# A fused attention and MLP block on one core: the start's loads in another order, the keys' weights in two transposed halves, and a new written-out order

## The chip, the cores and the metric

One core of a Trainium2 chip. The time is device microseconds of one execution; the kernel before takes 173.94 us (median of 3 runs, 173.92 to 173.96).

## The reference, cut to what matters

```python
def _A_ref(x, wqkv, w_phi, wo):            # S=2048, D=512, H=32 heads of 16
    qkv = (x @ wqkv).reshape(B, S, 3, H, Dh).transpose(2, 0, 3, 1, 4)
    q, k, v = qkv[0], qkv[1], qkv[2]
    pq = einsum("bhsd,hdf->bhsf", q, w_phi);  pk = einsum("bhsd,hdf->bhsf", k, w_phi)
    phi_q = concatenate([softmax(pq), softmax(-pq)]);  phi_k = the same of pk
    kv  = einsum("bhsf,bhsd->bhfd", phi_k, v);         z = sum of phi_k over s
    num = einsum("bhqf,bhfd->bhqd", phi_q, kv);        den = phi_q . z + 1e-6
    return (num / den) @ wo
def _B_ref(x, w1, b1, w2):                 # F=1792
    h = x @ w1 + b1
    return (h * tanh(softplus(h))) @ w2    # mish
xn = layernorm(x)
return x + _A_ref(xn, ...) + _B_ref(xn, ...)
```

## The kernel before, in words

The 2048 tokens are 16 tiles of 128, in 4 groups of 4. All data is bf16, sums are fp32. Each head's 16x16 feature map is folded into the projection: `fold` (L156) multiplies the transposed columns of `wqkv` (tile `wT`, loaded by a transposing DMA in `load_turned`, L143) with a block-diagonal `Wbd`, so that logits come straight from the normalised tokens. The keys' folded weights are `wkp`, the queries' `wqp`. `wT[:, j, kt*128:...]` is read by fold number `kt`, four matmuls each; folds 0 and 1 read its columns 0 to 255, folds 2 and 3 the others, and these columns are rows of `wqkv`.

Group 0 of the tokens is normalised tile by tile and turned by TensorE (`first_turn`, L560); the later groups are turned by DMA (`ln_turn_dma`, L186). Twelve matmuls on constants (`warm`, L513) stand ahead of everything on TensorE.

The whole order is written out by hand in the string `STEPS`; the schedule is manual, each engine runs its part of the steps in this order, and only semaphores for data and buffers hold it back. A number behind `@` is the PSUM bank (six, numbered 0 to 5; one double bank more is used in turn by wide logits, the accumulation and the attends). The steps:

- `LS i`, `RS i`, `AZ i`, `TP i`, `TC i`: statistics (DVE), reciprocal root (POOL), centring (DVE), turn (TensorE) and copy of tile i of group 0. `LN g`, `AP g k`: the same for group g, the turn by DMA from SP.
- `WB`: `Wbd`. `PB`, `CB`: the bias turned by TensorE (L533) and copied. `KM`: a mask.
- `F0 kt`, `FD kt`: fold of the keys' weights and its copy; `F`, `FC` for the queries. `WT` loads the queries' weights.
- `LP`: first logits, tiles 0 and 1 interleaved (L209). `L s i`, `LC s i`: logits of stage s (0 to 3 keys, 4 to 7 queries), tile i, and their copy. `WL`: two more of them in the double bank. `V t`, `VC t`: values.
- `H u`, `M u`: hidden units, 128 of 1792 for one group, u from 0 to 55, and mish on ScalarE.
- `E s l` extremes for the softmaxes (DVE, l = 0, 1 for the two signs), `X s k` exponential (ScalarE), `S s k` row sums (DVE, L305). Keys: `R` inverse of the sums (`v` on DVE, `a` through logarithm and exponential on ScalarE), `N` normalises, `A g k` accumulates kv. `KV` masks it. Queries: `W` weighs one softmax against the other (they share a denominator) and turns the features by DMA (`turn`, L295, tiles `qT`).
- `Q h i`, `G h i`, `C h`: attend (TensorE), gather to SBUF (ScalarE), division by the denominator (DVE) and a turn by DMA (L458). `O t`: second layer of the MLP, 14 matmuls; `P t`: output projection into the same bank; `Y t`: residual (DVE, L477) and store. `OH`, `PH`, `YH`: the last tile in two parts.
- `DX g`, `DW i`: loads of tokens, of `wo` (3) and `w2` (2).

ScalarE holds one table at a time, that of mish or that of exponential and logarithm; a change loads the other (`table`, L138).

The loads at the start stand ahead of the steps (L483 to L493), most on SP's queue, three on ACT's: `wsrc`, tile 1 of the tokens and the bias.

Of the kernel before, what the change touches and what calls it, by code (L numbers as in the profile page):

```python
# [23 lines left out]
STEPS = """
LS 0; RS 0; DX 2; LS 1; WB; RS 1; AZ 0; TP 0 @0; F0 0 @1; F0 1 @2; AZ 1; FD 0 v; TP 1 @3; TC 1 v; LS
2; PB @4; RS 2; TC 0 a; LS 3; RS 3; FD 1 a; AZ 2; F0 2 @5; F0 3 @0; FD 2 a; FD 3 a; LP i @1,2; KM;
DX 3; AZ 3; V 0 @3; LC 0 0 a; TP 2 @5; V 1 @0; TC 2 a; TP 3 @1; VC 0 a; LC 0 1 v; TC 3 v; CB; L 0 2
@5; L 0 3 @2; LC 0 3 a; LN 1; H 0 @3; H 1 @1; H 2 @4; M 0; LC 0 2 a; H 3 @2; M 1; M 2; M 3; VC 1 a;
E 0 0; H 4 @3; H 5 @5; AP 1 0; H 6 @1; H 7 @4; M 4; H 8 @2; M 5; H 9 @0; M 6; M 7; H 10 @3; M 8; M
9; M 10; AP 1 1; H 11 @5; E 0 1; V 4 @1; X 0 1; WL 1; LN 2; V 6 @4; VC 4 a; X 0 0; L 1 0 @2; L 1 3  # L30
@0; LC 1 0 a; V 5 @3; LN 3; VC 5 a; H 12 @1; WL 2; H 13 @2; VC 6 a; S 0 0; LC 1 3 a; M 11; V 3 @3; M
12; M 13; H 14 @4; H 15 @0; H 16 @5; H 17 @1; VC 3 a; M 14; H 18 @2; M 15; M 16; M 17; LC 1 2 a; H
19 @3; AP 2 0; AP 2 1; AP 3 0; L 2 0 @4; LC 2 0 a; L 2 1 @0; LC 2 1 a; V 2 @5; S 0 1; L 2 2 @1; M
18; LC 1 1 a; M 19; H 20 @4; LC 2 2 a; AP 3 1; H 21 @0; WT; H 22 @2; M 20; VC 2 a; R 0 1 v; L 2 3
@3; H 23 @1; R 0 0 v; N 0 1; M 21; N 0 0; H 24 @4; M 22; LC 2 3 a; F 0 @5; F 1 @0; E 1 0; E 1 1; M
23; M 24; F 2 @2; E 2 0; E 2 1; FC 0 a; H 25 @3; H 26 @1; FC 1 a; H 27 @4; M 25; M 26; L 3 2 @5; FC
2 a; M 27; V 7 @0; L 3 3 @3; V 11 @1; F 3 @2; L 3 0 @4; LC 3 0 v; LC 3 2 a; L 3 1 @5; A 0 0; X 1 0;
X 1 1; A 0 1; LC 3 3 a; FC 3 v; S 1 0; V 8 @4; LC 3 1 a; VC 7 a; L 4 0 @2; E 3 0; VC 8 a; LC 4 0 a;
L 4 1 @3; LC 4 1 a; L 4 3 @5; VC 11 a; L 4 2 @0; X 2 0; V 9 @4; L 5 0 @2; H 28 @3; H 29 @1; VC 9 a;
LC 4 2 v; M 28; M 29; H 30 @0; H 31 @4; H 32 @3; M 30; H 33 @1; H 34 @0; M 31; M 32; M 33; M 34; H  # L40
35 @4; M 35; H 36 @3; M 36; S 1 1; LC 4 3 a; R 1 0 v; E 3 1; LC 5 0 a; N 1 0; R 1 1 v; H 37 @1; H 38
@0; H 39 @4; H 40 @3; H 41 @5; H 42 @2; S 2 0; A 1 0; M 37; N 1 1; M 38; M 39; M 40; A 1 1; M 41; M
42; X 3 0; L 6 3 @1; L 5 2 @0; V 10 @4; VC 10 a; L 5 1 @3; LC 5 2 a; L 6 0 @5; E 4 0; E 4 1; X 2 1;
S 3 0; V 15 @2; VC 15 a; V 13 @4; VC 13 a; LC 6 0 a; R 2 0 a; S 2 1; DW 3; R 3 0 a; X 3 1; L 6 1 @0;
LC 5 1 a; DW 2; N 3 0; N 2 0; L 5 3 @2; O 0 @4; S 3 1; V 12 @5; V 14 @3; LC 6 1 a; LC 5 3 a; O 1 @0;
L 6 2 @2; R 2 1 a; N 2 1; VC 14 a; LC 6 3 a; VC 12 v; R 3 1 a; N 3 1; X 4 0; A 2 0; S 4 0; LC 6 2 a;
A 2 1; A 3 0; W 4 0 v; X 4 1; H 43 @3; M 43; A 3 1; H 44 @1; H 45 @5; M 44; H 46 @2; M 45; H 47 @3;
M 46; M 47; H 48 @1; KV; H 49 @5; H 50 @2; Q 0 0; M 48; M 49; G 0 0; M 50; H 51 @3; H 52 @1; H 53
@5; S 4 1; W 4 1 v; M 51; M 52; H 54 @2; H 55 @3; Q 0 1; M 53; E 5 0; E 5 1; M 54; E 6 0; L 7 0 @1;
M 55; G 0 1; C 0 a; X 5 0; LC 7 0 a; L 7 1 @5; X 5 1; O 2 @2; O 3 @3; LC 7 1 a; L 7 2 @1; LC 7 2 a;  # L50
S 5 0; Q 1 0; L 7 3 @5; G 1 0; E 6 1; W 5 0 a; P 0; P 1; Y 0; Q 1 1; O 4 @1; G 1 1; LC 7 3 a; O 5
@4; S 5 1; Q 2 0; O 6 @5; C 1 a; P 2; G 2 0; W 5 1 v; Y 1; Q 2 1; P 3; O 7 @0; E 7 0; X 6 0; S 6 0;
G 2 1; Q 3 0; C 2 a; G 3 0; Y 2; Y 3; X 6 1; O 8 @2; Q 3 1; W 6 0 v; E 7 1; S 6 1; P 4; P 5; G 3 1;
C 3 a; Q 4 0; X 7 0; Y 4; W 6 1 v; X 7 1; S 7 0; O 9 @3; O 10 @1; G 4 0; Q 4 1; P 6; P 7; G 4 1; Y
5; Y 6; C 4 a; Q 5 0; W 7 0 a; G 5 0; O 11 @4; Q 5 1; Y 7; O 12 @5; S 7 1; G 5 1; C 5 a; Q 6 0; G 6
0; O 13 @0; Q 6 1; G 6 1; W 7 1 v; P 8; P 9; Q 7 0; C 6 a; G 7 0; P 10; P 11; Y 8; Q 7 1; G 7 1; O
14 @2; Y 9; Y 10; C 7 a; P 12; P 13; OH 0 @3; PH 0; Y 11; P 14; OH 1 @1; PH 1; Y 12; Y 13; YH 0; Y
14; YH 1
"""


# [1 line left out]
def kernel(  # L63
# [19 lines left out]
    FT = F // P  # L83
# [53 lines left out]
            tables[0] = name  # L137
            nc.scalar.preload_act_table_set(name)  # L138

    def load_turned(base_col):  # L140
# [2 lines left out]
        nc.sync.dma_start_transpose(out=wT[:], in_=A_wqkv[:, base_col : base_col + D])  # L143
# [345 lines left out]
    nc.sync.dma_start(x_sb[:, 2:4, :], x_v[:, 2:4, :])
    nc.sync.dma_start(wv[:], wqkv_v[:, :, 2 * D : 3 * D])  # L490
# [165 lines left out]
```

## Time and profile before

| | |
|---|---|
| median of 3 runs | 173.94 us (173.92 to 173.96) |
| the profiled execution | 174.0 us |
| its span, first to last instruction | 172.3 us |
| granted TensorE clock | 1.000 |
| TensorE busy | 168.7 us, 1039 matmuls |
| VectorE, ScalarE busy | 143.2 us, 119.5 us |
| moved by DMA | 18.02 MB |

The span is what the profile's views cover; 1.7 us of the execution lie around it. Busy time counts overlapping instructions of one engine once. A matmul's end is modelled and lies some 0.16 us after the start of the next one in a row of back-to-back matmuls. "SPq" and "ACTq" are the DMA issues of these engines; "to landing" is the time from the start of the issue until the data is there.

### The profile page before, as it was taken

Reading aid. Unit: us, or ns where it says so; the run is one execution under the profiler, and the core shown is the slowest. Engines: PE = TensorE matmul, PEld = TensorE weight load, DVE = VectorE, ACT = ScalarE, POOL = GpSimd, SP = SyncE. Lnnn points to the kernel's source line nnn. Section 1 sums busy time; section 2 is a strip of 40 time slices with the busy share of each in tenths; the row PEclk is TensorE's granted clock in tenths of the full one; section 3 lists DMA queues with packets and bytes.
Section 4 is the critical chain, followed back from the end, with each engine's and each line's share of the span. In section 5 each row is a group of like instructions: output and inputs, shape, how many; then the busy total and the mean of one; then the engine's idle time right before and its main releaser. Section 6 shows DMA issues by size and latency. Waiting matters only on the chain.

```text
span 172.3 us, 2713 instructions
## 1 busy us (share of the span) xinstructions
PE 168.7 (98%) x1039; PEld 82.4 (48%) x1039; DVE 143.2 (83%) x221; ACT 119.5 (69%) x192; POOL 9.4 (5%) x26
## 2 busy tenths in 40 slices
PE   8999999999999999999999999999999999999993
PEld 2554444444545444454446544444444545445452
DVE  2878998999997999979999999799988996844433
ACT  2446889979899998989999988974063883414200
POOL 4332205000000000000000000000000000000000
PEclk9999999999999999999999999999999999999999
DMA  5999350199930000000000363023974749885641
GB/s 98 269 377 365 82 98 0 37 189 207 366 120 0 0 4 0 0 0 0 4 0 0 64 118 66 12 51 67 150 152 93 150 95 144 172 168 100 173 134 61
DMA packets 44953, 18.02 MB, mean 105 GB/s; under 512 B 37004, under 2 KB 44940, under 8 KB 44940
## 3 DMA queue, kind: packets, MB, share of 16 engines
q1 hardware_dynamic: 44096, 17.60, 44.5%
q10 hardware_dynamic: 844, 0.25, 0.6%
q8 instruction: 8, 0.13, 0.3%
q14 instruction: 5, 0.04, 0.1%
HBM read 6.84 MB, written 2.10 MB: 52 GB/s over the span
## 4 chain that ended last, share of the span: by engine, by line
PE 95%; DMA 3%; SPq 0%; DVE 0%; issue 0%
PE po L463 28%; PE ph L228 28%; PE pl L194 14%; PE po L470 8%; PE pv L194 8%; DMA wT<-in_A_wqkv_dram 3%; PE pnd L418 2%; PE pkv L387 2%; PE pfold L156 1%; PE pwide L194 1%; PE pl L209 1%; PE ptr L560 0%; SPq L483 0%; DVE x_sb L477 0%; PE pb L533 0%
## 5 line engine op out<-in xcount | busy, mean ns | idle before, releaser
L463 PE MATMUL po<-w_sb,acts 128*128 128x512 bf16 (+2 forms) x238 | 50.7, 366 | 0.0
L228 PE MATMUL ph<-xnT,w_sb 128*128 128x512 bf16 x224 | 50.1, 379 | 0.0
L239 ACT ACTIVATE acts<-ph,b1f 128x512 bf16<-128x512 f32 x56 | 37.2, 694 | 4.6 <-PE ph L228 4.4
L305 DVE TENSOR_REDUCE s<-e 128x128 f32<-128x2048 bf16 x16 | 36.4, 2279 | 2.5 <-ACT e L288 2.5
L228 PEld LDWEIGHTS <-w_sb 128*128 128x128 bf16 x224 | 21.7, 98 | 25.5
L463 PEld LDWEIGHTS <-acts 128*128 128x128 bf16 x238 | 22.3, 98 | 24.1
L288 ACT ACTIVATE e<-e 128x2048 bf16<-128x2048 bf16 x16 | 30.3, 1908 | 0.0
L194 PEld LDWEIGHTS <-xnT 128*128 128x128 bf16 x184 | 17.6, 98 | 20.1 <-DMA wv<-in_A_wqkv_dram 0.2
L252 ACT CAST p_sb<-pl 128x512 bf16<-128x512 f32 x27 | 15.4, 587 | 5.5 <-PE pl L194 4.7
L433 ACT COPY ds<-pnd 128x32 f32<-128x32 f32 x16 | 2.9, 183 | 23.5 <-PE pnd L418 23.5
L194 PE MATMUL pv<-wv,xnT 128*128 128x512 bf16 x64 | 16.1, 379 | 0.0
L477 DVE TENSOR_TENSOR x_sb<-po,x_sb 128x512 bf16<-128x512 f32 (+2 forms) x17 | 10.9, 654 | 5.7 <-PE po L470 5.7
L470 PE MATMUL po<-wqk,xnT 128*128 128x512 bf16 (+2 forms) x68 | 15.5, 366 | 0.0
L194 PE MATMUL pl<-wqk,xnT 128*128 128x512 bf16 x64 | 15.3, 379 | 0.0
L170 DVE BATCH_NORM_STATS2 stats<-x_sb 128x6 f32<-128x512 bf16 x16 | 10.1, 679 | 4.3 <-DMA x_sb<-in_A_x_dram 4.3
L263 DVE TENSOR_TENSOR m<-m 128x512 bf16<-128x512 bf16 (+1 forms) x32 | 11.5, 358 | 1.1
L194 PE MATMUL pl<-wkp,xnT 128*128 128x512 bf16 x48 | 11.7, 379 | 0.0
L263 DVE TENSOR_TENSOR m<-p_sb 128x1024 bf16<-128x1024 bf16 x16 | 10.9, 682 | 0.2 <-ACT p_sb L252 0.2
L272 DVE TENSOR_TENSOR e<-p_sb,m 128x2048 bf16<-128x2048 bf16 x8 | 9.8, 1226 | 1.4 <-PE pkv L387 1.1
L272 DVE TENSOR_TENSOR e<-m,p_sb 128x2048 bf16<-128x2048 bf16 x8 | 9.8, 1225 | 0.3
L340 DVE TENSOR_TENSOR e<-e,r 128x2048 bf16<-128x2048 bf16 x8 | 9.6, 1215 | 0.0
L138 ACT ACT_TABLE_LOAD x7 | 9.0, 1283 | 0.1
(62 smaller groups left out, 131.4 us busy)
## 6 DMA issues: line engine op xcount, KB each, us to landing
out_dram<-x_sb SPq DMA_DIRECT2D x15, 128.0 KB, 2.0
w_sb<-in_B_w_dram SPq DMA_DIRECT2D x2, 896.0 KB, 7.8
x_sb<-in_A_x_dram SPq DMA_DIRECT2D x3, 512.0 KB, 10.0
w_sb<-in_B_w_dram SPq DMA_DIRECT2D x2, 640.0 KB, 8.8
wv<-in_A_wqkv_dram SPq DMA_DIRECT2D x1, 512.0 KB, 4.5
wqk<-in_A_wo_dram SPq DMA_DIRECT2D x1, 512.0 KB, 4.6
w_sb<-in_B_w_dram SPq DMA_DIRECT2D x1, 512.0 KB, 9.6
x_sb<-in_A_x_dram SPq DMA_DIRECT2D x1, 256.0 KB, 3.2
```

Of the source, the lines that this page charges most:

```text
L170: nc.vector.bn_stats(stats[:, i, :], xs[:, i, :])
L194: nc.tensor.matmul(pp, lhsT=xnT[:, t, kt, :], rhs=w[:, kt, :], start=(kt == 0), stop=(kt == KT - 1),)
L228: nc.tensor.matmul(ph_of[u][:], lhsT=w1_sb[:, kt, f * P : (f + 1) * P], rhs=xnT[:, g * TPG : (g + 1) * TPG, kt, :], start=(kt == 0), stop= ...
L239: nc.scalar.activation(acts[:, f, g * 512 : (g + 1) * 512], ph_of.pop(u)[:], ACT.Mish, bias=b1f[:, f : f + 1])
L252: copy(p_of[s][:, i, :], pl_of.pop((s, i)))
L263: nc.vector.tensor_tensor(out=m[:], in0=src[:, :, 0:half], in1=src[:, :, half : 2 * half], op=op)
L272: nc.vector.tensor_tensor(out=e_of[s][:].rearrange("p t j l c -> p (t j) l c")[:, :, pl, :].rearrange("p t (c e o) -> p t c e o", e=8, o=2 ...
L288: nc.scalar.activation(v, v, ACT.Exp)
L305: nc.vector.reduce_sum(t[:], pair(s, k).rearrange("p t j l (c e) -> p (t j l c) e", e=16), axis=AX.X)
L463: nc.tensor.matmul(po_of[t, c.stop][:, c], lhsT=acts[:, f, t * P : (t + 1) * P], rhs=w2_sb[:, f, c], start=(f == 0), stop=False,)
L470: nc.tensor.matmul(po_of[t, c.stop][:, c], lhsT=oT_of[t // 2][:, t % 2 * 4 + j, :], rhs=wo_sb[:, j, c], start=False, stop=(j == 3),)
L477: nc.vector.tensor_tensor(out=y, in0=po_of.pop((t, c.stop))[:, c], in1=y, op=ALU.add)
```

## The change

Three things at the start. SP loads the first four tiles of tokens (0, 1, then 2 and 3 together) ahead of the keys' weights; tile 1 leaves ACT's queue. The keys' weights come in two transpositions of 256 rows of `wqkv`, so that folds 0 and 1 wait for the first alone. And the bias is turned first on TensorE, ahead of tile 0.

```diff
-    def load_turned(base_col):
+    def load_turned(base_col, *rows):
         wT = lnp.tile([P, 4, 512], BF16, name="wT", tag="xn")
-        nc.sync.dma_start_transpose(out=wT[:], in_=A_wqkv[:, base_col : base_col + D])
+        for r in rows:
+            nc.sync.dma_start_transpose(out=wT[:, :, r], in_=A_wqkv[r, base_col : base_col + D])
         return wT
...
-    nc.sync.dma_start(x_sb[:, 0, :], x_v[:, 0, :])
-    wT_of = {0: load_turned(D)}
+    for t in (slice(0, 1), slice(1, 2), slice(2, 4)):
+        nc.sync.dma_start(x_sb[:, t, :], x_v[:, t, :])
+    wT_of = {0: load_turned(D, slice(0, 256), slice(256, 512))}
     with nc.allow_non_contiguous_dma(reason="tiny w_phi load"):
         nc.scalar.dma_start(wsrc[:], wphi_v)
-    nc.scalar.dma_start(x_sb[:, 1, :], x_v[:, 1, :])
     nc.scalar.dma_start(b1b[:], b1_v[:, :])
-    nc.sync.dma_start(x_sb[:, 2:4, :], x_v[:, 2:4, :])
     nc.sync.dma_start(wv[:], wqkv_v[:, :, 2 * D : 3 * D])
...
-    wT_of[1] = load_turned(0)
+    wT_of[1] = load_turned(0, slice(0, D))
```

`w2` comes in two pieces and not three, and its step `DW 2` stands elsewhere in the order. Buffers: the row sums get 6 and not 3, the inverses `r2` 3 and not 2, `r` 1 and not 2; logarithms are written over their source, so the tile `log` is gone.

```diff
-        t = s_of[s, k] = smx.tile([P, 128], FP32, name="s", bufs=3)
+        t = s_of[s, k] = smx.tile([P, 128], FP32, name="s", bufs=6)
...
-    def log(src, n):
+    def log(v):
         table("natural_log_exp_and_others")
-        t = smx.tile([P, 128], FP32, name="log")
-        nc.scalar.activation(t[:, 0:n], src, ACT.Ln)
-        return t[:, 0:n]
+        nc.scalar.activation(v, v, ACT.Ln)
+        return v
...
-        r2 = r_of[s, k] = smx.tile([P, 128, 2], BF16, name="r2")
+        r2 = r_of[s, k] = smx.tile([P, 128, 2], BF16, name="r2", bufs=3)
...
-        r = smx.tile([P, 128], BF16, name="r")
+        r = smx.tile([P, 128], BF16, name="r", bufs=1)
...
-            for f in (slice(0, 5), slice(5, 10), slice(10, FT)):
+            for f in (slice(0, 7), slice(7, FT)):
```

The string `STEPS` is new throughout: the same 433 steps in another order, with other banks and other choices of `v` and `a` for some copies. Its begin, and the stretches that the prediction speaks of:

```diff
-LS 0; RS 0; DX 2; LS 1; WB; RS 1; AZ 0; TP 0 @0; F0 0 @1; F0 1 @2; AZ 1; FD 0 v; TP 1 @3; TC 1 v; LS
-2; PB @4; RS 2; TC 0 a; LS 3; RS 3; FD 1 a; AZ 2; F0 2 @5; F0 3 @0; FD 2 a; FD 3 a; LP i @1,2; KM;
-DX 3; AZ 3; V 0 @3; LC 0 0 a; TP 2 @5; V 1 @0; TC 2 a; TP 3 @1; VC 0 a; LC 0 1 v; TC 3 v; CB; L 0 2
+KM; LS 0; LS 1; RS 0; AZ 0; PB @0; DX 2; TP 0 @1; WB; F0 0 @2; FD 0 a; F0 1 @3; FD 1 a; RS 1; AZ 1;
+TP 1 @4; F0 2 @5; TC 0 v; FD 2 a; TC 1 v; LS 2; RS 2; F0 3 @1; FD 3 a; LS 3; AZ 2; RS 3; AZ 3; LP i
+@2,4; V 1 @3; CB; TP 2 @5; V 0 @1; VC 1 v; TP 3 @0; LC 0 0 a; LC 0 1 a; TC 3 v; TC 2 a; L 0 2 @2; LC
...
+@2; R 1 0 a; VC 5 a; X 2 0; S 1 1; LC 3 3 a; LC 4 0 a; L 4 1 @3; LC 4 1 v; R 1 1 a; L 3 1 @4; LC
+3 1 v; H 32 @0; H 33 @3; H 34 @5; H 35 @4; L 4 3 @1; M 31; M 32; M 33; M 34; H 36 @2; M 35; M 36; H
...
+@1; LC 7 0 a; L 7 1 @3; L 7 3 @2; G 0 0; Q 0 1; G 0 1; O 3 @1; LC 7 1 a; C 0 a; X 5 1; LC 7 3 a; Q 1
...
+7 0 a; P 6; P 7; G 5 0; Y 6; S 7 1; Q 5 1; G 5 1; O 12 @4; Q 6 0; C 5 a; W 7 1 v; Y 7; G 6 0; P 8; Y
+8; P 9; Q 6 1; O 13 @5; G 6 1; Q 7 0; P 10; C 6 v; P 11; Y 9; Y 10; G 7 0; Q 7 1; G 7 1; C 7 a; O 14
+@0; P 12; P 13; Y 11; OH 0 @1; PH 0; P 14; OH 1 @3; Y 12; Y 13; YH 0; Y 14; PH 1; YH 1
```

On SP's queue the second token load of the steps (`DX 3`) now stands behind both turns of group 1, and `wo` (`DW 3`) between the two turns of group 3.

More of the change, by code (lines that the diff above doesn't have):

```diff
@@ L24 @@
 STEPS = """
-LS 0; RS 0; DX 2; LS 1; WB; RS 1; AZ 0; TP 0 @0; F0 0 @1; F0 1 @2; AZ 1; FD 0 v; TP 1 @3; TC 1 v; LS
-2; PB @4; RS 2; TC 0 a; LS 3; RS 3; FD 1 a; AZ 2; F0 2 @5; F0 3 @0; FD 2 a; FD 3 a; LP i @1,2; KM;
-DX 3; AZ 3; V 0 @3; LC 0 0 a; TP 2 @5; V 1 @0; TC 2 a; TP 3 @1; VC 0 a; LC 0 1 v; TC 3 v; CB; L 0 2
-@5; L 0 3 @2; LC 0 3 a; LN 1; H 0 @3; H 1 @1; H 2 @4; M 0; LC 0 2 a; H 3 @2; M 1; M 2; M 3; VC 1 a;
-E 0 0; H 4 @3; H 5 @5; AP 1 0; H 6 @1; H 7 @4; M 4; H 8 @2; M 5; H 9 @0; M 6; M 7; H 10 @3; M 8; M
@@ L30 @@
[L30 to L58, printed above, removed]
+KM; LS 0; LS 1; RS 0; AZ 0; PB @0; DX 2; TP 0 @1; WB; F0 0 @2; FD 0 a; F0 1 @3; FD 1 a; RS 1; AZ 1;
+TP 1 @4; F0 2 @5; TC 0 v; FD 2 a; TC 1 v; LS 2; RS 2; F0 3 @1; FD 3 a; LS 3; AZ 2; RS 3; AZ 3; LP i
@@ new lines @@
+@2,4; V 1 @3; CB; TP 2 @5; V 0 @1; VC 1 v; TP 3 @0; LC 0 0 a; LC 0 1 a; TC 3 v; TC 2 a; L 0 2 @2; LC
+0 2 a; H 0 @4; M 0; L 0 3 @5; LC 0 3 a; LN 1; H 1 @3; H 2 @0; E 0 0; VC 0 a; H 3 @2; H 4 @4; H 5 @5;
+M 1; AP 1 0; AP 1 1; DX 3; M 2; M 3; H 6 @1; E 0 1; LN 2; M 4; M 5; H 7 @3; H 8 @0; H 9 @2; M 6; M
+7; M 8; X 0 0; V 2 @4; H 10 @5; S 0 0; L 1 0 @1; LC 1 0 v; V 4 @3; X 0 1; LN 3; VC 2 a; WL 1; H 11
+@0; WL 2; VC 4 a; H 12 @4; H 13 @3; M 9; M 10; AP 2 0; R 0 0 v; M 11; M 12; M 13; AP 2 1; AP 3 0; DW
@@ new lines @@
+3; AP 3 1; WT; H 14 @1; H 15 @2; L 1 3 @5; LC 1 3 a; LC 1 1 a; LC 1 2 a; E 1 0; S 0 1; E 1 1; M 14;
+M 15; H 16 @0; H 17 @4; M 16; M 17; H 18 @3; H 19 @5; H 20 @1; M 18; H 21 @2; H 22 @0; H 23 @4; H 24
+@3; M 19; M 20; H 25 @5; M 21; M 22; H 26 @1; M 23; M 24; H 27 @2; M 25; H 28 @0; N 0 0; H 29 @4; M
+26; M 27; H 30 @3; R 0 1 v; L 2 2 @5; M 28; M 29; M 30; X 1 0; V 3 @1; VC 3 v; L 2 0 @2; L 3 0 @0;
+LC 3 0 a; LC 2 0 a; LC 2 2 a; A 0 0; L 2 3 @4; LC 2 3 a; L 2 1 @3; N 0 1; F 0 @1; F 1 @0; LC 2 1 a;
@@ new lines @@
+F 2 @2; S 1 0; E 2 0; A 0 1; FC 2 a; FC 1 a; F 3 @5; V 6 @4; FC 0 a; FC 3 a; V 10 @3; X 1 1; VC 6 a;
+V 11 @2; V 7 @0; VC 7 a; E 2 1; L 4 0 @1; VC 11 a; L 3 3 @5; L 3 2 @4; V 5 @0; VC 10 a; LC 3 2 v; H
+31 @2; R 1 0 a; VC 5 a; X 2 0; S 1 1; LC 3 3 a; LC 4 0 a; L 4 1 @3; LC 4 1 v; R 1 1 a; L 3 1 @4; LC
+3 1 v; H 32 @0; H 33 @3; H 34 @5; H 35 @4; L 4 3 @1; M 31; M 32; M 33; M 34; H 36 @2; M 35; M 36; H
+37 @0; M 37; H 38 @3; M 38; H 39 @5; H 40 @4; H 41 @2; H 42 @0; M 39; M 40; H 43 @3; S 2 0; N 1 0; L
@@ new lines @@
+4 2 @5; R 2 0 v; E 3 0; M 41; N 1 1; H 44 @4; M 42; M 43; H 45 @2; A 1 0; LC 4 3 a; A 1 1; E 3 1; LC
+4 2 a; E 4 0; E 4 1; V 9 @0; M 44; V 15 @3; M 45; X 2 1; S 2 1; V 8 @1; VC 8 a; L 6 0 @5; X 3 1; DW
+2; N 2 0; O 0 @4; LC 6 0 a; L 5 0 @2; X 3 0; S 3 0; VC 9 a; S 3 1; L 6 1 @1; VC 15 a; LC 5 0 a; V 14
+@5; VC 14 a; L 5 1 @0; H 46 @3; L 5 3 @2; LC 5 1 a; O 1 @5; LC 6 1 a; R 3 0 a; N 3 0; R 2 1 a; LC 5
+3 a; V 12 @0; L 5 2 @1; V 13 @2; N 2 1; X 4 1; S 4 1; VC 12 a; A 2 0; R 3 1 a; L 6 3 @0; A 2 1; LC 5
@@ new lines @@
+2 a; VC 13 a; L 6 2 @1; A 3 0; X 4 0; LC 6 3 a; N 3 1; A 3 1; H 47 @2; LC 6 2 a; M 46; E 5 0; M 47;
+H 48 @0; H 49 @1; H 50 @3; M 48; H 51 @2; M 49; M 50; S 4 0; M 51; KV; W 4 0 v; E 5 1; H 52 @0; M
+52; H 53 @1; H 54 @3; H 55 @2; W 4 1 v; O 2 @0; Q 0 0; M 53; M 54; E 6 0; M 55; X 5 0; S 5 0; L 7 0
+@1; LC 7 0 a; L 7 1 @3; L 7 3 @2; G 0 0; Q 0 1; G 0 1; O 3 @1; LC 7 1 a; C 0 a; X 5 1; LC 7 3 a; Q 1
+0; O 4 @3; W 5 0 v; G 1 0; E 6 1; S 5 1; L 7 2 @2; LC 7 2 a; Q 1 1; G 1 1; C 1 a; P 0; Y 0; P 1; O 5
@@ new lines @@
+@2; X 6 0; X 6 1; Q 2 0; O 6 @4; W 5 1 v; G 2 0; S 6 0; Y 1; W 6 0 v; Q 2 1; G 2 1; C 2 a; P 2; Y 2;
+P 3; Q 3 0; G 3 0; O 7 @5; Q 3 1; O 8 @0; G 3 1; Q 4 0; E 7 0; P 4; P 5; E 7 1; Y 3; Y 4; C 3 a; G 4
+0; Q 4 1; X 7 0; O 9 @1; X 7 1; S 6 1; W 6 1 v; G 4 1; O 10 @3; Y 5; O 11 @2; Q 5 0; S 7 0; C 4 a; W
+7 0 a; P 6; P 7; G 5 0; Y 6; S 7 1; Q 5 1; G 5 1; O 12 @4; Q 6 0; C 5 a; W 7 1 v; Y 7; G 6 0; P 8; Y
+8; P 9; Q 6 1; O 13 @5; G 6 1; Q 7 0; P 10; C 6 v; P 11; Y 9; Y 10; G 7 0; Q 7 1; G 7 1; C 7 a; O 14
@@ L316, in power @@
         )
-    def log(src, n):
+    def log(v):
         table("natural_log_exp_and_others")
-        t = smx.tile([P, 128], FP32, name="log")
-        nc.scalar.activation(t[:, 0:n], src, ACT.Ln)
-        return t[:, 0:n]
+        nc.scalar.activation(v, v, ACT.Ln)
+        return v
     def invert(s, k, how):
         t = s_of.pop((s, k))
-        r2 = r_of[s, k] = smx.tile([P, 128, 2], BF16, name="r2")
+        r2 = r_of[s, k] = smx.tile([P, 128, 2], BF16, name="r2", bufs=3)
         if how == "a":
-            power(r2[:], log(t[:], 128), 128, -1.0)
+            power(r2[:], log(t[:]), 128, -1.0)
             return
-        r = smx.tile([P, 128], BF16, name="r")
+        r = smx.tile([P, 128], BF16, name="r", bufs=1)
         with nc.allow_low_precision("the softmaxes are bf16"):
@@ L350, in weigh @@
         if how == "a":
-            t4 = log(t[:], 128).rearrange("p (t l c) -> p t l c", l=2, c=4)
+            t4 = log(t[:]).rearrange("p (t l c) -> p t l c", l=2, c=4)
             nc.vector.tensor_tensor(
@@ L446, in combine @@
         if how == "a":
-            power(f[:], log(d, 64), 64, -1.0)
+            power(f[:], log(d), 64, -1.0)
         else:
```

## The prediction

> **What bounds the kernel now.** I read the page first: the busy shares and the slices.
>
> ```profile
> PE 168.7 (98%) x1039; PEld 82.4 (48%) x1039; DVE 143.2 (83%) x221; ACT 119.5 (69%) x192; POOL 9.4 (5%) x26
> ...
> PE   8999999999999999999999999999999999999993
> ...
> DMA  5999350199930000000000363023974749885641
> ```
>
> TensorE is busy in every slice but the first and the last; the DMA engines are full in the first 17 us. Next the waits of TensorE, over the whole span:
>
> ```profile
> PE warm L513 <- PEq L640: 0.8, 1, 0.8
> ```
>
> It is the only one: from 0.83 us on its row shows no wait. Then the chain of waits in order of time; columns are start, length, what:
>
> ```profile
> 1.25 5.36 DMA wT<-in_A_wqkv_dram
> 6.65 0.62 PE pfold L156 x8
> 7.61 0.55 PE pfold L156 x8
> 8.16 1.73 PE pl L209 x8
> 9.88 0.86 PE pv L194 x4
> ...
> 169.41 0.24 PE po L470 x4
> 169.67 0.29 DVE x_sb L477
> ```
>
> The only piece that is not TensorE's own work is the transposed load of the keys' weights. So TensorE's work sets the end, and a change that leaves its matmuls alone (1039 before and after) can move it only by moving the moment at which the gapless stretch begins, by tearing a hole in it, or behind the last matmul. The ceiling on a gain is thus small. I looked at the start in the timeline (start, length, engine):
>
> ```profile
> 0.83 5.28 PE L513 MATMUL warm<-const-bfloat16-1.0 128*128 128x512 bf16 x12 [0.83 <-PEq L640]
> ...
> 1.25 3.12 SPq L143 DMA_TRANSPOSE wT<-in_A_wqkv_dram  x1
> ...
> 4.42 0.56 SPq L489 DMA_DIRECT2D x_sb<-in_A_x_dram  x1
> ...
> 5.04 0.46 SPq L490 DMA_DIRECT2D wv<-in_A_wqkv_dram  x1
> ...
> 6.03 0.53 PE L560 MATMUL ptr<-ident,xn 128*128 128x128 bf16 x4
> ...
> 6.65 0.45 PEld L156 LDWEIGHTS <-wT 128*128 128x128 bf16 x8 [0.27 <-DMA wT<-in_A_wqkv_dram]
> ...
> 8.00 1.89 PE L209 MATMUL pl<-wkp,xnT 128*128 128x512 bf16 x8
> ```
>
> The warming matmuls start 0.427 apart, so TensorE is free at 0.83 + 12 x 0.427 = 5.96. Until the first logits (LP) at 8.00 it does 1.65 of work: two turns of a tile (0.36, 0.37), two groups of eight folds (0.40, 0.41), the bias (0.11). It wastes 8.00 - 5.96 - 1.65 = 0.39: 0.27 for the weights, the rest mostly for tile 0. This 0.39 is all that the change can win at the start.
>
> **The start, part by part.** Tiles: SP now issues tile 0, 1 and 2-3 (0.40, then about 0.5 and 0.56 by the rows of L487 and L489, with 0.06 between) before the weights, whose first half starts near 2.42, not 1.25. Tiles 2 and 3 land near 4.5, not 7.6 (4.42 + 3.2 in the list of issues): nobody waits for them now, so this is worth nothing by itself. Tile 1 leaves the ACT queue (landed 4.4 there); near 4 now. The work on tiles 0 and 1 on VectorE stays ready by about 6.5 (Wbd, now after tile 0, by 6.0).
>
> The weights: when does the second half (b) land, since TensorE must then do eight folds (0.41) before LP, with 0.1 for noticing the load and for LP's first weights? Two ways to it.
> From the bytes: the whole landed at 6.61 (1.25 + 5.36), behind tiles 0 and 1; the DMA engines were at 0.6 to 1.4 of one in every stretch from 1.5 to 6.0. Now 256 KB (tiles 2-3) go in front; at 365 GB/s (the DMA row at 6.5 to 6.75) that is 0.7: b lands at 7.3.
> From the issue: the trace has both kinds, a whole (tile wT) and the features' turns (tile qT); min, median and max of the issue in ns, then of issue to landing.
>
> ```profile
> L143 SPq DMA_TRANSPOSE wT<-in_A_wqkv_dram x2: 1819/2470/3120, 1.2 to 38.0; - x2
> ...
> DMA to landing us min/median/max: 5.0/5.2/5.4
> ```
>
> ```profile
> L295 SPq DMA_TRANSPOSE qT<-e x16: 1233/1318/2382, 96.4 to 155.1; - x16
> ...
> DMA to landing us min/median/max: 3.1/3.2/4.1
> ```
>
> A half has as many elements as one qT, which costs 1.24 alone and 1.34 behind another. The whole cost 1.82 at 38.0 but 3.12 at the start: 1.30 more. If those 1.30 are the queue pushing back against full DMA engines, the two halves end at 2.42 + 2.6 = 5.0, and b lands 1.9 later as qT does: 6.9, or bound by the bytes, 7.3. If they are a price of the first transposition, they stay: issue ends at 6.3, b at 6.3 + 1.9 = 8.2.
> I take 7.4, close to the bytes, since the first whole landed only 0.4 later after its issue began than the second did, although it was issued 1.30 slower: its data came while it was being issued. Ends 6.9 and 8.4.
> [...]
>
> LP then starts at 7.4 + 0.1 + 0.41 = 7.9, against 8.00: **-0.1**. Below 7.1 nothing more is won, since LP can't start before 5.96 + 1.65 = 7.61. The four copies of the folds are now all ACT's, 0.47 apart: with b early the last ends at 6.83 + 3 x 0.47 + 0.59 = 8.83, just before LP's last pair at 7.61 + 6 x 0.216 = 8.90; behind b = 7.4 they have 0.2 more room. The bias turned first stands at the head of TensorE's queue, with everything behind it; its 3.5 KB were issued on ACT at 1.83 and now at 1.28 and the tile beside it landed in 3.1, so it is there by 4.4 and costs 0.11 as before.
>
> Behind LP: V 1 needs wv. It landed at 9.54 before, with 768 KB of other loads ahead; the sum of bytes ahead is the same, so 9.5 at the latest against LP's end near 9.6: nothing. The first hidden layer needs w1's first part, landed 11.94; now wanted near 12.8 instead of 13.4. Nothing. Tokens 4-7 (13.4), turned by DMA: statistics 2.66, exponents' first half 2.98, two tiles centred 0.66, so issued at 19.75, landed 3.3 later at 23.05; the first logits on them start at 24.0.
>
> **The rest of the order.** TensorE's steps follow from sums: 0.863 for four 512-wide matmuls, 3.02 for a second layer (O), 0.51 for half an accumulation, 0.26 for an attend (Q); 2.24 for turns and folds, 0.87 for the queries' folds. Checked on before: the sum to the first Q is 95.20, it started at 101.46, so starts are sum + 6.26, and results are there 0.16 later. I laid VectorE's and ScalarE's new order against this, by their starts apart: extremes 2.98, row sums 2.20, normalising 1.14, residual 0.60, exponential 1.80, mish 0.58, copies 0.47 (ACT) and 0.60 (DVE), table load 1.29. VectorE's total goes from 144.6 to 145.3, ScalarE's from 111.8 to 110.8; both keep 7 table loads. TensorE waits nowhere in it, but four places are thin:
> - H 36 wants the bank that mish 31 empties, behind a table load. V 5 ends at 59.74; copy, exponential, two copies, an inversion (0.67), the load and mish sum to 5.9: 65.7 against 66.5. Room 0.8.
> - Q 0 1 wants the gather of Q 0 0, which stands behind the copy of L 7 0 (ready 110.08): 111.3 against 111.6. Room 0.3.
> - O 12 takes O 6's bank, which the residual Y 6 empties; P 6 ends at 148.5, Y 6 at 149.2, O 12 starts at 149.45 (sum of 56 H, 32 L, 16 V, 12 O, 8 P, 12 Q, 8 halves of accumulation and the folds: 143.2). Room 0.2. In the order before Y 6 stood a whole O earlier.
> - O 13 likewise behind Y 7, which is now behind the last row sums and W 7 1: 154.15 against 154.7. Room 0.6; and W 7 1's turn lands at 156.75 for Q 7 0 at 157.7.
>
> Nothing comes late in steady running, and I take **0** for it; a slip goes through to the end one for one, as no later idle time takes it up. One late row sum (2.28) at the thinnest would cost 2.1.
>
> Edits with one answer: more buffers and logarithms in place take waits away from engines that are not the bound; w2 "later" is not later on the queue, as it stands right behind the queries' transposition in both programs and that one waits for group 2's turns, centred by 34; two pieces for three save 0.5 of idle SP time. The last combination on VectorE costs 1.4 there for ScalarE's 0.5, and its turn lands 2.7 before P 12. The last ten steps of TensorE and the final stores keep their order, so the 2.65 behind the last matmul stays. All 0.
>
> Sum: -0.1 on the profiled 174.0 (span 172.3 and 1.7 around it) gives 173.9; the median of the runs is 0.06 lower, so 173.85.
>
> **The rivals.**
> 1. The second half is late (slower). The 1.30 of the first transposition is a fixed price. Then b lands at 8.2, LP starts at 8.7, +0.7: 174.6. For it: the second whole transposition went out in 1.82 on the same queue. Against: the landing argument above. It decides from b = 7.8 on (+0.3).
> 2. The halves overlap fully (faster): b by 7.1, first half folded at once behind tile 0's turn, LP at 7.61: -0.39, so 173.55, the floor. For it: qT pairs 1.3 apart each land in 3.2. Against: 256 KB more in front.
> 3. A thin place tears: +0.6 or so (174.5), at most 2.1.
> 4. The clock. Warming matmuls ran 0.427 apart, those after 8.00 0.216: TensorE reaches its full pace at about 6.1. The new order leaves it idle for up to 0.6 between the second and third fold; if the full pace came only after it, LP's eight would take twice 1.73: +1.7, 175.5. Against it: the 0.27 of idle time at 6.4 to 6.65 did no harm, and the granted clock reads 1.00. [...]
> 5. The change does not do what it says: true for w2 (above), worth 0.
>
> **How the numbers follow.** A difference of 0.2% (0.35 us) is about what a measurement of this kernel tells from no change. Forecast, b between 7.1 and 7.8 and no tear: 0.45, all within that bound. Rival 2: 0.18, and all the chance of faster. Rival 1: 0.25; rival 3: 0.08; rival 4: 0.04; together 0.37 for slower. The forecast's own range is 173.55 to 174.25. The range for 8 in 10 runs from the floor of rival 2, 173.5, to b = 8.4 (LP at 8.9, +0.9): 174.9; outside are the clock and the larger tears.
>
> **What would show it.** Right: the two wT transpositions issued near 2.4 and 3.7, TensorE waiting for the second once, by 0.5 or so, LP starting at 7.7 to 8.2, and no wait of TensorE behind it; the span shifts by what LP shifts. Wrong: a first issue of over 2 us and LP after 8.4; a wait for a residual at O 12 or for a gather at Q 0 1; matmuls 0.43 apart after the folds; or a span that moves by more than LP does.

## The result: slower by 0.4 to 0.6 us

The changed kernel took 174.50 us (median of 7 runs, 174.11 to 175.37) against 173.94 for the kernel before on the same chip: ratio 1.0043, 95% interval [1.0023, 1.0064]. Run again later it took 174.22 (10 runs, 173.71 to 174.60), ratio 1.0024 [1.0012, 1.0036]. Over all 17 runs its median is 174.41. It is slower, within the range given, on the side of the first rival; the forecast was no change.

The profiled execution took 174.5, with a span of 172.8. First the changed kernel's page, busy shares and slices:

```profile
PE 167.6 (97%) x1039; PEld 82.1 (48%) x1039; DVE 144.0 (83%) x223; ACT 118.9 (69%) x189; POOL 9.3 (5%) x26
...
PE   8699999999999999999999999999999999999993
...
DMA  5999082099960000000000006608479186948641
```

TensorE is less than full in the second slice (4.3 to 8.6 us), which was full before, and in no other slice between the first and the last. Its waits, over the whole span, are now three where there was one:

```profile
PE pfold L156 <- DMA wT<-in_A_wqkv_dram: 1.1, 2, 0.9
PE warm L511 <- PEq L638: 0.8, 1, 0.8
PE ptr L558 <- DVE xn L181: 0.6, 1, 0.6
```

The timeline of the start (start, length, engine) has the places:

```profile
2.18 3.07 SPq L143 DMA_TRANSPOSE wT<-in_A_wqkv_dram  x2
...
5.30 0.58 SPq L488 DMA_DIRECT2D wv<-in_A_wqkv_dram  x1
...
5.61 0.40 PE L558 MATMUL ptr<-ident,xn 128*128 128x128 bf16 x4 [0.60 <-DVE xn L181]
...
6.94 0.45 PEld L156 LDWEIGHTS <-wT 128*128 128x128 bf16 x8 [1.11 <-DMA wT<-in_A_wqkv_dram]
...
7.95 0.62 PE L156 MATMUL pfold<-Wbd,wT 128*128 128x128 bf16 x8 [0.16 <-DMA wT<-in_A_wqkv_dram]
...
8.40 1.89 PE L209 MATMUL pl<-wkp,xnT 128*128 128x512 bf16 x8
...
10.13 1.03 PE L194 MATMUL pv<-wv,xnT 128*128 128x512 bf16 x4
```

The first half of the weights lands at 6.9, later than the whole did (6.61), the second at 7.90. LP starts at 8.40 instead of 8.00, the first values (`pv`) at 10.13 instead of 9.72. The chain of waits names the same load. Its last piece starts at 170.20 instead of 169.67, so 0.53 later:

```profile
2.18 1.32 SPq L143
3.55 4.35 DMA wT<-in_A_wqkv_dram
8.57 1.73 PE pl L209 x8
...
170.20 0.29 DVE x_sb L476
```

From the first values to the last residual it is 160.07 us here and 159.95 before. So 0.41 of the 0.53 arises before 10.13, and 0.12 in one hole behind it: tokens 4 to 7 land late,

```profile
14.59 2.47 DVE L170 BATCH_NORM_STATS2 stats<-x_sb 128x6 f32<-128x512 bf16 x4 [1.66 <-DMA x_sb<-in_A_x_dram]
```

1.16 later than before (13.43). So the exponential ahead of the copy `VC 2` on ScalarE comes late too, and H 12, which takes the bank that this copy empties, starts at 28.82 where 28.70 was due.

### The profile page after: what moved, and what is told of

The parts are those of the page before. It is cut to its first block, busy times and chain, and to the rows that moved or that the text cites. A ratio compares the mean times of both kernels' runs of the same rounds, so it can differ in the third digit from the quotient of the medians.

```text
span 172.8 us, 2709 instructions
## 1 busy us (share of the span) xinstructions
PE 167.6 (97%) x1039; PEld 82.1 (48%) x1039; DVE 144.0 (83%) x223; ACT 118.9 (69%) x189; POOL 9.3 (5%) x26
## 4 chain that ended last, share of the span: by engine, by line
PE 94%; DMA 3%; SPq 1%; issue 0%; DVE 0%
PE ph L228 28%; PE po L462 28%; PE pl L194 14%; PE po L469 8%; PE pv L194 8%; DMA wT<-in_A_wqkv_dram 3%; PE pnd L417 2%; PE pkv L386 2%; PE pwide L194 1%; PE pl L209 1%; PE pfold L156 1%; SPq L143 1%; SPq L483 1%; PE ptr L558 0%; DVE x_sb L476 0%
## 5 line engine op out<-in xcount | busy, mean ns | idle before, releaser
L239 ACT ACTIVATE acts<-ph,b1f 128x512 bf16<-128x512 f32 x56 | 36.3, 704 | 4.8 <-PE ph L228 4.5
L252 ACT CAST p_sb<-pl 128x512 bf16<-128x512 f32 x26 | 14.3, 589 | 5.4 <-PE pl L194 4.8
L194 PE MATMUL pl<-wqk,xnT 128*128 128x512 bf16 x64 | 15.9, 379 | 0.0
L194 PE MATMUL pv<-wv,xnT 128*128 128x512 bf16 x64 | 15.6, 379 | 0.0
L218 ACT CAST vext<-pv 128x512 bf16<-128x512 f32 x14 | 7.7, 599 | 2.3 <-PE pv L194 2.3
```

What stands on the lines that cost most here:

```text
L194: nc.tensor.matmul(pp, lhsT=xnT[:, t, kt, :], rhs=w[:, kt, :], start=(kt == 0), stop=(kt == KT - 1),)
L239: nc.scalar.activation(acts[:, f, g * 512 : (g + 1) * 512], ph_of.pop(u)[:], ACT.Mish, bias=b1f[:, f : f + 1])
L252: copy(p_of[s][:, i, :], pl_of.pop((s, i)))
```

## The experiments

The question was which edit costs the time and by what. The theories: **A**, the 256 KB of tiles 2 and 3 ahead of the weights delay them. **B**, two transpositions cost more than one of the same bytes. **C**, TensorE's idle time at the start costs pace. **D**, the new order tears. In all tables LP and V are the starts of the first logits and of the first values in the profiled execution, and the rest is what lies between V and the last residual. A ratio compares a kernel with the kernel before as it ran beside it: 173.94 for the changed kernel, 173.90 for e1 to e3 and e5, 173.87 for e4 and e6 to e8, 173.85 for the later ones.

**Parts of the change taken back.** `e1_old_loads` has the new order and buffers with the loads of before; `e2_one_whole` the change with one transposition; `e3_tiles23_behind` the change with tiles 2 and 3 behind the halves; `e5_new_loads_old_order` is the kernel before with the change's edits of the loads, and nothing else of it.

```diff
# e2_one_whole, against the changed kernel (e1 puts the tiles back as well)
-    wT_of = {0: load_turned(D, slice(0, 256), slice(256, 512))}
+    wT_of = {0: load_turned(D, slice(0, D))}
# e3_tiles23_behind, against the changed kernel
-    for t in (slice(0, 1), slice(1, 2), slice(2, 4)):
+    for t in (slice(0, 1), slice(1, 2)):
...
+    nc.sync.dma_start(x_sb[:, 2:4, :], x_v[:, 2:4, :])   # ahead of wv
```

> The changed kernel with the loads of before (tile 0, the keys' weights whole, tile 1 on ACT's queue, tiles 2-3 behind the weights); the new order and buffers stay. Theory A (the time is lost because the four tiles stand ahead of the weights): the weights land near 6.6, the first logits start at 8.0, the span is 172.3 and the time 173.9 to 174.0. Theory B (two transpositions cost a pause of their own): the same here, 173.9. Theory C (TensorE stands idle from 4.9 to 6.9 and its clock suffers in some executions): 173.9, and the scatter of the changed kernel (174.1 to 175.4) closes. Theory D (the new order tears behind the start): stays above 174.3.

> The changed kernel with the keys' weights in one transposition, still behind the four tiles. A: the whole lands at 2.2 + 5.4 = 7.6 or later, first logits at 8.1 to 8.4, no change or 0.2 less than the changed kernel (174.2 to 174.5). B: the pause of about 0.5 between the halves is gone, the whole lands by 7.4, first logits at 7.9, 174.0. D: 174.5 as before.

> The changed kernel with tiles 2-3 behind the two halves instead of ahead of them (256 KB fewer in front, tile 1 stays on SP). A: the second half lands 0.7 earlier, at 7.2, first logits at 7.75, 173.8. B: only the 0.5 of issue is won, the second half lands at 7.4 to 7.6, 174.1. D: 174.4 or more, whatever the first logits do.

> The kernel before, its order and buffers, with the loads of the changed kernel (four tiles ahead, two halves). A and B: the same late second half, first logits near 8.4, 0.4 to 0.6 slower than before, 174.4. C: slower with the same scatter. D: 173.9 to 174.1, as the old order does not tear.

| | median (range), runs | ratio [95%] | LP | V | rest |
|---|---|---|---|---|---|
| before | 173.94 (173.61 to 174.02), 7 | | 8.00 | 9.72 | 159.95 |
| changed | 174.50 (174.11 to 175.37), 7 | 1.0043 [1.0023, 1.0064] | 8.40 | 10.13 | 160.07 |
| e1 | 173.99 (173.66 to 174.52), 11 | 1.0007 [0.9998, 1.0016] | 7.54 | 9.41 | 159.96 |
| e2 | 174.43 (174.15 to 174.86), 5 | 1.0037 [1.0025, 1.0050] | 8.12 | 9.96 | 159.95 |
| e3 | 174.34 (174.19 to 175.56), 10 | 1.0032 [1.0017, 1.0048] | 7.16 | 9.94 | 159.95 |
| e5 | 174.43 (174.18 to 175.03), 6 | 1.0039 [1.0025, 1.0053] | 7.69 | 9.76 | 159.97 |

The rest is 159.95 to 160.07 whatever the order. e1 shows that the whole new order, the buffers and `w2` are worth nothing; D falls, but for the 0.12 at H 12. e5 shows the other side: the loads alone bring the loss into the old order. Taking back one of the two edits of the loads takes nothing back that can be told from the scatter.

e3 shows why. With tiles 2 and 3 behind, LP starts at 7.16, earlier than in any other kernel here, and it helps little:

```profile
7.16 1.92 PE L209 MATMUL pl<-wkp,xnT 128*128 128x512 bf16 x8
9.94 0.81 PE L194 MATMUL pv<-wv,xnT 128*128 128x512 bf16 x3 [0.87 <-DMA wv<-in_A_wqkv_dram]
```

The values wait 0.87 for `wv`, which lands at 9.9. V starts when LP has ended (1.73 to 1.87 later) and `wv` is there, whichever is later. In the profiled executions of these six kernels `wv` landed between 9.1 and 9.9.

**Each edit alone, in the kernel before.** `e6_split_only`: two halves; `e7_tile1_on_sp_only`: tile 1 on SP ahead of the weights; `e8_tiles23_ahead_only`: tiles 2 and 3 ahead of the one transposition.

```diff
# e6_split_only, against the kernel before
-    wT_of = {0: load_turned(D)}
+    wT_of = {0: load_turned(D, slice(0, 256), slice(256, 512))}
# e7_tile1_on_sp_only, against the kernel before
     nc.sync.dma_start(x_sb[:, 0, :], x_v[:, 0, :])
+    nc.sync.dma_start(x_sb[:, 1, :], x_v[:, 1, :])
     wT_of = {0: load_turned(D)}
...
-    nc.scalar.dma_start(x_sb[:, 1, :], x_v[:, 1, :])
# e8_tiles23_ahead_only, against the kernel before
     nc.sync.dma_start(x_sb[:, 0, :], x_v[:, 0, :])
+    nc.sync.dma_start(x_sb[:, 2:4, :], x_v[:, 2:4, :])
     wT_of = {0: load_turned(D)}
...
-    nc.sync.dma_start(x_sb[:, 2:4, :], x_v[:, 2:4, :])
```

> The kernel before with the keys' weights in two halves, and nothing else changed. In the six profiles so far the stretch from the first values' matmul to the last instruction is 159.95 to 160.07 us, so the time hangs on when that matmul starts: when the first logits are done and the values' weights (wv) have landed. Theory B (a second transposition costs a pause of its own, 0.3 to 0.5): wv lands at 9.9, first values at 10.0, 174.2 to 174.4. Theory A (only what stands ahead counts): wv at 9.5, first values at 9.7, 173.9.

> The kernel before with tile 1 loaded by SP ahead of the keys' weights instead of by ACT beside them, and nothing else changed. If the 0.5 of issue that the weights start later is what counts (A'): weights issued at 1.7, wv 0.4 later, first values at 10.0 to 10.1, 174.3. If only the bytes ahead of wv count, which are the same: 173.9.

> The kernel before with tiles 2-3 loaded by SP ahead of the keys' weights, tile 1 still on ACT, weights whole. A': weights issued 0.5 later and behind 256 KB, whole landed at 7.1 to 7.3, first logits 8.5 to 8.7, first values at 10.2 to 10.4, 174.5. If only the bytes ahead of wv count: wv still at 9.5, and the first values follow the first logits, 174.2 at most.

| | median (range), runs | ratio [95%] | LP | V | rest |
|---|---|---|---|---|---|
| e6 | 174.13 (173.85 to 175.35), 12 | 1.0022 [1.0005, 1.0038] | 7.65 | 9.41 | 160.02 |
| e7 | 173.86 (173.58 to 174.15), 12 | 1.0001 [0.9991, 1.0011] | 7.78 | 9.51 | 159.95 |
| e8 | 174.25 (174.08 to 174.50), 12 | 1.0024 [1.0014, 1.0033] | 8.22 | 9.95 | 160.03 |

Tile 1's move costs nothing. Tiles 2 and 3 ahead cost 0.4 by themselves. So they are a cause, but in e8 not in the way that A says: the weights landed at 6.67, only 0.06 later than before. Tile 1, still on ACT's queue beside them, landed at 4.80 instead of 4.39, its statistics stand on VectorE ahead of tile 0's centring, and the first turn came late:

```profile
PE ptr L560 <- DVE xn L181: 0.8, 1, 0.8
```

In e2, where tile 1 comes by SP ahead of tiles 2 and 3, it is the weights that come late, at 6.94, and TensorE waits 0.31 for them. The split alone costs 0.25, although the profiled execution, the fastest of the twelve at 173.85, starts LP earlier than before; a second profile of it stands below.

**The clock.** `e4_busy_between` puts six small matmuls on constants into the idle time behind tile 0's turn, in the changed kernel.

```diff
-TP 0 @1; WB; F0 0 @2;
+TP 0 @1; WB; JK; F0 0 @2;     # JK: six 128x128 matmuls on constants
```

> The changed kernel with six more matmuls on constants (128 wide, 0.3 to 0.7 us) between the turn of tile 0 and the first fold, where TensorE stood idle for 0.94; they compute nothing. Theory C (idle time there holds the clock down in some executions): the highest times (174.9, 175.4) go and the median falls below 174.3. A, A' and B: 174.4 to 174.6 and the same scatter.

It took 174.50 (174.10 to 175.07, 12 runs), ratio 1.0035 [1.0022, 1.0047], with LP at 8.30 and V at 10.03. C falls: TensorE's idle time was not the price. Its rest of 160.31 has two holes: H 12 waits as in the changed kernel, and the first hidden unit starts 0.20 late, at 13.27, as the first part of `w1` landed only at 13.22.

**How much a further transposition costs.** `e9_four_quarters` is the kernel before with four transpositions of 128 rows; `e12_split_again` is e6 and `e11_after_again` the changed kernel, both run again for a second profile; `e10_order_tile1_sp` keeps the new order and what cost nothing in the loads: tiles 0 and 1 on SP, the whole weights, then tiles 2 and 3.

```diff
# e9_four_quarters, against the kernel before
-    wT_of = {0: load_turned(D)}
+    wT_of = {0: load_turned(D, *(slice(i, i + P) for i in range(0, D, P)))}
# e10_order_tile1_sp, against the changed kernel
-    for t in (slice(0, 1), slice(1, 2), slice(2, 4)):
-        nc.sync.dma_start(x_sb[:, t, :], x_v[:, t, :])
-    wT_of = {0: load_turned(D, slice(0, 256), slice(256, 512))}
+    nc.sync.dma_start(x_sb[:, 0, :], x_v[:, 0, :])
+    nc.sync.dma_start(x_sb[:, 1, :], x_v[:, 1, :])
+    wT_of = {0: load_turned(D, slice(0, D))}
...
+    nc.sync.dma_start(x_sb[:, 2:4, :], x_v[:, 2:4, :])
```

> The kernel before, with the keys' weights loaded in four transpositions of 128 rows each where it has one of 512; nothing else is changed. Theory B (each further transposition at the start costs a pause of its own in the data): two halves alone took 0.25 us more than before, so three further pieces take 0.5 to 0.8 more, 174.4 to 174.7, with the first values starting later than 9.72 and a wider scatter above the median. Theory A (only the 256 KB put ahead of the weights cost time): within 0.1 of before, 173.8 to 174.0, since the bytes and their order stay.

> The kernel before with its keys' weights in two halves of 256 rows and nothing else, unaltered from the run above, to firm up the price of the split and to see a second execution of it. Theory B: 174.05 to 174.25, and in a profiled execution that is slower than 174.0 the second half or the values' weights land later than in the one seen (first values at 9.41). Theory A: 173.85 to 173.95.

> The changed kernel again, unaltered, for a second profiled execution and its scatter. If the loss is the later start of the first values (theories A and B): its profiled time is the start of the first values plus 164.2 to 164.5, and the median 174.4 to 174.6. If a hole in the steady part decides (theory D): executions differ in a hole behind the first values by more than 0.3.

> The changed kernel with its new order and buffers, but with the loads of tile 0, tile 1 and the whole keys' weights in this order on the sync queue and tiles 2 and 3 behind them; the weights in one transposition. If the loss lies in the split and in tiles 2 and 3 standing ahead, and the rest is worth nothing: 173.85 to 174.0, no different from before, the first values starting at 9.4 to 9.75. If the new order itself costs something that the old loads hid: 174.2 or more, with a start of the first values no later than before.

| | median (range), runs | ratio [95%] | LP | V | profiled time |
|---|---|---|---|---|---|
| e9 | 176.25 (175.82 to 176.45), 4 | 1.0140 [1.0126, 1.0155] | 8.62 | 11.87 | 176.45 |
| e12 | 174.25 (174.02 to 175.35), 11 | 1.0036 [1.0022, 1.0051] | 7.31 | 9.77 | 174.25 |
| e11 | 174.22 (173.71 to 174.60), 10 | 1.0024 [1.0012, 1.0036] | 7.85 | 9.57 | 173.86 |
| e10 | 173.88 (173.68 to 173.98), 11 | 1.0004 [0.9995, 1.0013] | 7.77 | 9.62 | 173.97 |

Four pieces cost 2.4 us, far more than the 0.5 to 0.8 that B had for them; A expected nothing. The waits of e9's TensorE show what is late:

```profile
PE pv L195 <- DMA wv<-in_A_wqkv_dram: 1.4, 1, 1.4
PE pfold L157 <- DMA wT<-in_A_wqkv_dram: 0.9, 2, 0.5
```

and its issues why (tile `wT`; min, median and max of the issue in ns, then issue to landing):

```profile
L144 SPq DMA_TRANSPOSE wT<-in_A_wqkv_dram x4: 1255/1268/1285, 1.2 to 5.2; - x4
...
DMA to landing us min/median/max: 2.9/3.4/3.9
```

A piece of 128 rows takes 1.27 of SP's time, a half 1.29 to 1.70, the whole 1.82 to 3.14. Four pieces keep SP until 6.46, so `wv` is issued at 7.14, 2.10 later than before, and lands late by as much and a little more:

```profile
7.14 4.68 DMA wv<-in_A_wqkv_dram
```

So the price of four pieces is mostly issue time. That of two is not: at the start two halves were issued in 2.66 to 3.07 together, the whole in 2.34 to 3.12. Here the amount of data that flows may count. The windows from 4.0 to 8.5 us hold the end of the transposition and plain loads behind it (last column: mean GB/s of all DMA), here e10 with one transposition, the changed kernel with two, and e9 with four:

```profile
4.00:8.50 4.50, 3.41 (x34) 2.05 (x33) 3.25 (x9) 1.42 (x3) 1.61 (x4) 1.00 1.14 272
```

```profile
4.00:8.50 4.50, 2.80 (x31) 1.75 (x29) 3.05 (x9) 1.12 (x3) 1.61 (x4) 1.00 1.19 222
```

```profile
4.00:8.50 4.50, 3.38 (x28) 1.73 (x27) 2.88 (x7) 1.65 (x3) 1.72 (x4) 1.00 0.51 111
```

Over all profiled executions with loads on one queue this is 254 to 273 with one transposition (before, e1, e2, e7, e8, e10), 222 to 258 with two (changed, e3, e4, e5, e6, e11, e12; the middle one 225), and 111 with four. With the same loads in front the comparison is closer. Behind four tiles it is 258 with one piece (e2) against 222 to 231 with two (changed, e4, e5, e11), behind two tiles 272 and 273 (e10, e7) against 224 (e3), but behind tile 0 alone 254 and 259 (before, e1) against 258 and 248 (e6, e12). The 33 GB/s between e2 and the middle one of its four partners are 150 KB over 4.5 us, or 0.4 us at the 361 to 377 GB/s that flow in these five from 8.5 to 13.0 us (an estimate). That is about the size of the changed kernel's loss. It does not explain the price of the split alone. What the kernels with halves share is a `wv` that lands later on the whole: at 9.06 to 9.50 behind one piece (six executions), at 9.36 to 9.90 behind two (seven).

While a whole is being loaded, stretches of half a microsecond reach 290 GB/s of all DMA (before, 5.0 to 5.5), but from its issue to its landing all DMA together moved 180 (before) to 232 GB/s (e8).

e12's profile, taken at its median time, shows the split alone at work: LP at 7.31, 0.7 earlier than before, and V at 9.77, no earlier (9.72), as TensorE waits 0.57 for `wv`:

```profile
4.58 5.14 DMA wv<-in_A_wqkv_dram
```

It took 5.14 to land where it took 4.5 before. So the early weights bring nothing. What they cost is not shown by this: of the 0.25 by which this execution is longer than the profiled one of before, 0.05 lies ahead of V, and the rest, between V and the last residual (0.11) and behind it (0.12), comes where e12 changes nothing. The price of the split alone stands on the runs (0.25 in e6, 0.40 in e12), and its place in the kernel stays open. e11 shows that the forecast's start does occur in the changed kernel: the second half lands at 7.34, LP starts at 7.85, and that execution takes 173.86.

```profile
7.39 0.62 PE L156 MATMUL pfold<-Wbd,wT 128*128 128x128 bf16 x8
7.85 1.89 PE L209 MATMUL pl<-wkp,xnT 128*128 128x512 bf16 x8
```

It is one of the fastest of its ten. In all profiled executions on one queue, time less V is 164.3 to 164.6. So 174.41, the median of all runs of the changed kernel, stands for a V of about 10.0, and before's 173.9 for 9.6.

e10 equals before: the order loses nothing and gains nothing, and no kernel tried beats the kernel before.

**Two queues.** `e15_two_queues` issues the second half on ACT's queue, tile 1 on SP's, in the kernel before.

```diff
         for i, r in enumerate(rows):
-            nc.sync.dma_start_transpose(out=wT[:, :, r], in_=A_wqkv[r, base_col : base_col + D])
+            (nc.scalar if i else nc.sync).dma_start_transpose(out=wT[:, :, r], in_=A_wqkv[r, base_col : base_col + D])
```

> The kernel before with its keys' weights in two halves, the first issued on SP's queue behind tiles 0 and 1, the second on ACT's queue right behind the small feature weights; tile 1, which stood on ACT's queue, goes on SP's (alone it was worth nothing). Both halves are issued by about 3.0 us, at the same time. If the price is the serial issue on one queue: the second half lands by 6.3, the values' weights, issued on SP near 3.6, by 9.3, and the time is that of before or up to 0.3 less, 173.5 to 173.9. If each transposition brings a pause in the data wherever it is issued: the first values start at 9.6 to 9.9 and the time is that of the split on one queue, 174.05 to 174.3. If two transpositions at a time get in each other's way: the halves land after 7.0 and the time is over 174.4.

It took 177.75 (175.78 to 179.03, 6 runs), ratio 1.019 [1.0153, 1.0227], and did not do what it was meant to: the two did not run side by side. The ratio leaves out the two longest. The timelines of SP and of ACT in its profiled execution, the longest of the six:

```profile
5.17 1.32 SPq L144 DMA_TRANSPOSE wT<-in_A_wqkv_dram  x1
```

```profile
1.29 1.31 ACTq L144 DMA_TRANSPOSE wT<-in_A_wqkv_dram  x1
```

ACT's piece, the second half, landed at 1.29 + 3.86 = 5.15. SP's issue before it had ended at 1.66; it issued the first half only at 5.17, 3.5 later and 0.02 behind that landing, with all its later loads behind it: `wv` went out at 7.16, 2.12 later than before. What holds SP back until then no run shows. So the run leaves open whether two halves at once would be faster.

Only part of its time is this late start. The six executions fall into three groups by their granted clock: 175.78 at 1.000, 177.59 to 177.84 at 0.990, 178.89 and 179.03 at 0.981. At the full clock, in one execution, two queues cost 1.9; what goes beyond that goes with TensorE's pace (last section).

What stays open is why a piece of 128 rows takes as long to issue as most halves (1.27 against 1.29 to 1.32), by what two pieces slow the loads behind them, and why executions of the kernels with halves differ more (up to 175.56) than those with a whole (up to 174.86 in those compared here). The granted clock does not part them, as it reads 1.000 in the longest: 175.56 (e3), 175.37 (changed) and 175.35 (e6 and e12). No profile of these is kept.

## Why the prediction was wrong

- **What bounds the kernel, and that only the start can move it: right.** All twelve kernels on one queue keep time = V + 164.3 to 164.6. (The DMA engines, read as full in the first 17 us, were at 0.54 up to 4.3, and at 0.00 to 1.83 in the quarter microseconds from 1.5 to 6.0.) One sign of being wrong showed: the span moved by 0.54, LP by 0.40.
- **The failed step is the term for the second half, b = 7.4.** The four profiled executions with the new loads had it at 7.2, 7.34, 7.80 and 7.90 (e5, e11, e4, changed), and the two late ones are the typical ones: their executions lie at the median (174.50) and 0.14 above it, the other two are the fastest of e5's six and the second fastest of e11's ten. The step from b to LP was right: 0.51 taken, 0.50 measured (7.90 to 8.40). Both parts of the estimate of b were off, in opposite directions. The 256 KB ahead were put at +0.7; with one transposition and tile 1 on SP (e2) the landing moved from 6.61 to 6.94, so +0.33. The split was put at 0, as the bytes stay the same; behind the same four tiles two halves landed 0.96 and 0.86 later than the whole in the changed kernel and e4 (0.40 and 0.24 in e11 and e5). So a term that was taken for nothing cost up to 0.96. By what the split delays the second half is not shown; a lower data rate is the likeliest (above).
- **The issue time was nearly right, the landing behind it was not.** Halves were issued in 1.32 and 1.70, so the 1.30 extra of the first transposition is no fixed price, as I argued against rival 1. But the half's own landing time, taken as 1.9 behind the end of its issue from the features' turns, was 2.65 (7.90 less 3.55 + 1.70), and 2.0 to 2.7 in the other profiles with halves.
- **The turning point of rival 1 (b = 7.8) was right**, and b lies there. Rival 1 had the sign and nearly the size (174.6), for another reason than the one given for it; that the number came so near is luck.
- **The ceiling of 0.39 and "V 1 needs wv: nothing" failed.** LP was taken for the only gate. LP's end and the landing of `wv` lie close together in the kernel before (9.72 and 9.50), so with `wv` landing as it did there an LP at 7.61, which would end at 9.34, gains 0.2 and not 0.39. e3, e5 and e12 run into that gate. The bytes ahead of `wv` were also miscounted, without effect: they are 1024 KB, not 768 (four tiles of 128 KB and 512 KB of weights), before and after.
- **"Tiles 2 and 3 ahead: worth nothing by itself" failed**: 0.4 alone (e8), and as much in the new order (e2 against e1). What these bytes push back was counted only against the halves, not against tile 1 (e8).
- **Tokens 4 to 7** landed 1.16 later than taken, and H 12 was missing among the thin places; that cost 0.12. In e11, the same kernel, they landed at 13.65, and the rest is 159.96. The first part of `w1`, taken at 11.94, landed at 13.06, just ahead of the first hidden unit at 13.17.
- **Order, buffers, `w2`, tile 1: 0, right** (e1, e7, e10). The four thin places held: Y 6 started at 149.02, took 0.69, and O 12 started at 149.94.
- **Rival 4, the clock: right that it does not act here** (0.9 and 0.6 of idle time, LP's matmuls still 0.216 apart). e15 shows nearly its price for LP: 1.61 where 1.7 was taken.

## What to carry to other kernels

Where a transposed load stands at the head of the queue, count its pieces, not only its bytes, because what is queued behind them pays: behind four pieces `wv` was issued 2.10 later (e9). Here four pieces cost 2.4 us, mostly in issue time, and two cost 0.25 to 0.4 without a longer issue. An early first piece buys nothing if the next operand stands behind them (e12: LP 0.7 earlier, V no earlier). Before an earlier start is counted as a gain, look up the landing of every load that the next two steps need; the second gate may be 0.2 us behind the first (9.50 and 9.72 in the kernel before). A start that differs by half a microsecond between executions of one program (LP at 8.40 and 7.85 in the changed kernel) needs more than one profile.
